# Late rows of the last two segments in the opening's pass, and three gate/up pairs moved into steps 58 to 60

## The chip, the cores and the metric

The kernel runs on one NeuronCore of a Trainium2 chip. The core has TensorE (PE, matrix products into PSUM), VectorE (DVE), ScalarE (ACT), GpSimd (POOL) and SyncE (SP), which here issues nearly all DMA transfers. The metric is the time of one execution on the device in microseconds. The profile is of one execution; its times count from the start of its span.

## The reference

Input x is 2048 rows of 640. The output is the sum of two residual parts:

```
h  = x + A(layernorm(x))
h2 = h + B(layernorm(h))
```

A is attention with a recurrent memory. The rows are cut into 64 segments of 32. Each segment is joined to 8 memory rows, and these 40 rows go through q, k and v products (32 heads of 128), masked softmax and the output product Wo. The first 8 output rows are the memory of the next segment, the other 32 are the segment's output. So the 64 segments follow one another strictly.

```
h = concatenate([mem, xs]);  q, k, v = h @ Wq, h @ Wk, h @ Wv
p = softmax(where(mask, q k^T * scale, -1e9));  o = (p @ v) @ Wo
mem = o[:8];  out = o[8:]
```

B is a gated feed-forward, `relu(x Wg) * (x Wu) @ Wd` with 1728 inner columns.

## The kernel before, in words

**Order.** The kernel lists its operations in program order with the buffers that each reads and writes (`add`, line 39). `solve` derives the waits, and each engine then runs its own operations in that order. SP is a queue too: a transfer that waits holds up all that SP has listed behind it.

**Segments and steps.** A PE pass has 32 columns of activations as its stationary operand, four column groups side by side, and streams the weights, 512 columns at a time: `project` (line 373), 40 matmuls for each of K, Q and V. Step s puts 8 memory rows and the first 24 rows of segment s into one pass. The other 8 rows of each segment, its late rows, do not wait for the memory. They are gathered for four segments at once in `act_e` (4 times 8 columns) and go through K, Q and V in a pass of their own. These passes are the filler of the steps: `extra_units` (line 797) gives each of three steps out of four one of the three passes for the next four segments, cut into three parts that PE runs between the products of the recurrence (`filler`, line 968); the fourth step runs the Wo product of late rows instead. Results go to `Ke`, `Qe` and `Ve`, two buffers each, used in turn by groups of four segments.

**Groups.** `place(s)` (line 454) gives buffer and column of a segment. Segments 0 and 1 are columns 2 and 3 of buffer 1, 2 to 5 are columns 0 to 3 of buffer 0, and so on; 62 and 63 are columns 0 and 1 of buffer 1. So the first and the last group hold two segments each, and half of their columns are empty. The opening (lines 727 to 778) normalises rows 0 to 63 (`ln1_load(-1)`), computes the first two groups while the weights arrive, and steps 58, 59 and 60 compute K, Q and V of the last.

**Fill.** `fill_of` (line 950) gives for each step a number of extra PE instructions: weight loads that could be left out, and 512-column matmuls cut in two. It changes no result.

**Feed-forward.** Rows are handled in four blocks of 512. `gate_up(b, j)` (line 847) is one pair: 5 gate and 5 up matmuls of 128 inner columns, a relu on ACT and a product on DVE into `hT`; 13 full pairs and a narrow tail (`Wt`) per block. `down_pair` (line 1145) is the product with Wd, two tiles of 128 rows at a time; its first part asks for `hT` chunks 0 to 11 and Wd pieces 0 to 3 at once. The weights of the feed-forward lie where Wq, Wk and Wv were, so they are loaded only from step 62 on, in pieces (`load_piece`, `load_down`), held in order by keys on `hT`. Block 0 needs no new attention rows: its normalised rows were written to DRAM (`xn2_d`) in steps 19 to 43 and are loaded at step 62. Its first four pairs are spread over step 63 and what follows, the others are in the loop at line 1217. That loop also runs the normalisation of block 1 (`ln2_front` on DVE and ACT, `ln2_back` as a DMA transpose on SP), starting at pair 5 (`at0`).

Of the kernel before, what the change touches and what calls it, by code (L numbers as in the profile page):

```python
# [146 lines left out]


def bass_sequential_preLN__memory_aug_recurrent_mem_tr__glu_gated_reglu__prompt_kernel(
    nc: bass.Bass,  # L150
    A_x: bass.AP,
    A_mem0: bass.AP,
    A_Wq: bass.AP,
    A_Wk: bass.AP,
    A_Wv: bass.AP,
    A_Wo: bass.AP,
    A_seg_len: bass.AP,
    B_x: bass.AP,
    B_W_gate: bass.AP,
    B_W_up: bass.AP,  # L160
    B_W_down: bass.AP,
    out: bass.AP,
):
    build_kernel(nc, A_x, A_mem0, A_Wq, A_Wk, A_Wv, A_Wo, A_seg_len, B_W_gate, B_W_up, B_W_down, out)


def build_kernel(nc, A_x, A_mem0, A_Wq, A_Wk, A_Wv, A_Wo, A_seg_len, B_W_gate, B_W_up, B_W_down, out):
# [20 lines left out]
    xn2_d = nc.dram_tensor("xn2_d", [128, DC, TB], BF16)  # L188
    attn_d = nc.dram_tensor("attn_d", [S, 4, DC * 32], BF16)

    es = ExitStack()
# [38 lines left out]
    Ko = ar.alloc("Ko", [128, H, 32], BF16)  # L230
    Ke = [ar.alloc(f"Ke{i}", [128, H, 32], BF16) for i in range(2)]
    Qo = ar.alloc("Qo", [128, H, M + SEG], BF16)
    Qe = [ar.alloc(f"Qe{i}", [128, H, 32], BF16) for i in range(2)]
    Ve = [ar.alloc(f"Ve{i}", [128, 8, VW], BF16) for i in range(2)]
    Vp = ar.alloc("Vp", [128, 8, VW], BF16)
# [32 lines left out]

    def ap(t, off, dims, p0=0, n=128):
        row = 1  # L270
        for s in t.shape[1:]:
            row *= s
        return bass.AP(t, p0 * row + off, [[row, n]] + dims)
# [148 lines left out]
    def n_rows(b):  # L422
        return 64 if b < 0 else min(128, S - 64 - 128 * b)

    def ln1_load(b, buf, key, eng="sp"):
        t0, n = (0, 64) if b < 0 else (64 + 128 * b, min(128, S - 64 - 128 * b))
        dma(buf[0:n, :], x_ap[t0:t0 + n, :], w=[key], eng=eng)

    def ln1_trans(b, buf, key, bk):
        transpose_rows(buf, key, 64 if b < 0 else min(128, S - 64 - 128 * b), bk)  # L430

    def ln1_back(b, src, r, eng):

        n = n_rows(b)

        def copy(dst, sl, w):
            if eng == "pool":
                add("pool", lambda p: p.tensor_copy(dst, sl), r=r, w=w)
            else:
                add("dve", lambda v: v.tensor_copy(dst, sl), r=r, w=w)  # L440
        if b < 0:
            for e in range(2):
                copy(act_r[1][:, 2 + e, :, M:32], src[:, :, SEG * e:SEG * e + RID], [("act", 1, "x", 2 + e)])
                copy(act_e[1][:, :, M * (2 + e):M * (3 + e)], src[:, :, SEG * e + RID:SEG * e + SEG], [("acte", 1)])
            return
        for j in range(n // SEG):
            copy(act_r[b % 2][:, j, :, M:32], src[:, :, SEG * j:SEG * j + RID], [("act", b % 2, "x", j)])
        for j in range(n // SEG):
            copy(act_e[b % 2][:, :, M * j:M * j + M], src[:, :, SEG * j + RID:SEG * j + SEG], [("acte", b % 2)])
# [3 lines left out]

    def place(s):
        return (s - 2) // 4 % 2, (s - 2) % 4

# [284 lines left out]

    row_stats(xt, ("xt",), 64)
    row_scale(xt, ("xt",), 64, xt, ("xt",))
    ln1_trans(-1, xt, ("xt",), P0)
# [29 lines left out]
    def first_values(chunks):  # L774
        for c in chunks:
            for (a, ks), bks in zip((PASSES[0], PASSES[2]), OB[2]):
                project(a, ks, 2, (0, 1), bks, (c,))
    first_values(range(2))

    GROUPS = ((0, 256), (256, 512), (512, 1024), (1024, 1536), (1536, FM))  # L780
    pieces = [(t, n, src, g, lo, hi) for g, (c0, c1) in enumerate(GROUPS)
              for n, (t, src) in enumerate(((Wg, B_W_gate), (Wu, B_W_up)))
              for lo, hi in (((0, 3), (3, DC)) if c1 - c0 == 512 else ((0, DC),))]

# [10 lines left out]
    WPARTS = (range(0, 8), range(8, 9), range(9, 16))  # L795

    def extra_units(s):
        p, r = 1 - place(s)[0], place(s)[1]
        if s == NSEG - 3:
            p = 1 - place(NSEG - 1)[0]  # L800
            j = 0
            a, ks = act_e[p], [("acte", p)]
        elif s < NSEG - 3 and r < 3:
            j = (1, 0, 2)[r]
            a, ks = act_e[p], [("acte", p)]
            if s < 0 or (s - 2) // 4 + 1 > (NSEG - 2) // 4:
                return None, None
        else:
            return None, None
# [140 lines left out]
    def fill_of(s):  # L950
        n = {1: 31, 2: 8, 57: 39, 61: 39, 62: 50, 63: 0}.get(s, FILL[s % 4])
        alone = min(n // 4, 3)
# [3 lines left out]
    for s in range(1, NSEG):  # L956
# [16 lines left out]
        if s > 0:  # L973
            a, ks = pass_act(s)
            held, parts = fill_of(s)
            for i in range(2):
                project(a, ks, 1, (i,), ((P2, P3)[i],), *WAYS[i], held=i == 1 and held[0], parts=parts[i])
# [48 lines left out]
        if last:  # L1026
# [4 lines left out]
            exp_x(s, 0)  # L1031
            gate_up(0, 0)
            scores(s, 1)
# [136 lines left out]
    def load_down(n):  # L1170
        lo, hi = 3 * n, min(3 * n + 3, FC - 1)
        r = [("Wdone", 1), ("hT", 0, n + 4)]
        dma(Wd[:, lo:hi, :], B_W_down[128 * lo:128 * hi, :].rearrange("(j p) d -> p j d", p=128), r=r, w=[("Wd", n)])
# [20 lines left out]
    rows(P3, s % 2, s - 1)  # L1194
    gate_up(0, 1)
    load_piece(("VM", 0, 3))
    load_piece(("hT", 0, 0))
    pv_x(s, P0)
# [3 lines left out]
    late_o(s)  # L1202
    load_piece(("hT", 0, 1))
    gate_up(0, 2)
    ln2_load(4)
    load_piece(("hT", 0, 2))
    load_piece(("hT", 0, 2))
    gate_up(0, 3)
    load_piece(("hT", 0, 3))
    load_piece(("hT", 0, 3))  # L1210
    rows(P2, (s + 1) % 2, s)
# [5 lines left out]
    for b in range(NBLK):  # L1217
        if 0 < b < NBLK - 1:
            for u in range(4):
                ln2_load(4 * (b + 1) + u)  # L1220
        at0 = 5 if b == 0 else 1
        for j in range(FC):
            if b or j > 3:
                gate_up(b, j)
            if b == 0 and 4 <= j < 7:
                load_piece(("hT", 0, j))
            if b == 0 and j in (5, 7):
                ln2_load(6 + (j - 5) // 2)
            if b == 0 and 4 <= j < 9:
                load_down(j - 4)  # L1230
            if b == 0 and j == 5:
                for q, src in enumerate((B_W_gate, B_W_up)):
                    for e in range(2):
                        r0 = FR * (q ^ e)
                        dma(Wt[:, e, :, r0:r0 + FR], src[:, FM:F].rearrange("(c p) f -> p c f", p=128),
                            r=[("Wdone", 0), ("hT", 0, 5)], w=[("Wt", q, e)])
            if b == 0 and j == 9:
                dma(h_rows[0][:, :, :], h_d[:, :].rearrange("(u p) d -> p u d", p=128), r=[("h_d", u) for u in range(4)] +
                    [("Wdone", 1), ("hT", 0, 9)], w=[("h", 0, u) for u in range(4)])
            if b + 1 < NBLK:  # L1240
                if j - at0 in (0, 2, 4, 6):
                    ln2_front(4 * (b + 1) + (j - at0) // 2)
                if j - at0 - 2 in (0, 2, 4, 6):
                    ln2_back(4 * (b + 1) + (j - at0 - 2) // 2, None)
        assert not pieces
# [65 lines left out]
```

## Time and profile before

| | |
|---|---|
| median of 3 runs | 1000.74 us (1000.2 to 1001.01) |
| the profiled execution | 999.84 us, span 998.1 us |
| one step (steps 2 to 60) | 11.9 to 12.3 us |
| opening, to the first matmul of step 1 | 56.8 us |
| steps 58, 59, 60, 61: first matmul at | 744.4, 756.4, 768.5, 780.5 us |
| step 63: first matmul at | 804.7 us |
| block 0: loop of pairs from, down product from | 826.1, 846.6 us |
| block 1: first pair at | 861.7 us |
| DMA moved | 73.3 MB, 44 GB/s from and to HBM over the span |

A row of the timeline is start, length, engine, line of the kernel, operation, tiles written and read, shapes and number. Matmuls overlap: the distance from start to start is what one costs, its length is the time until its last result. A row of the stage table is the stretch, its length, then busy time and instructions of PE, PEld (weight loads), DVE, ACT and POOL, the granted PE clock, the busy share of the DMA engines and GB/s. SPq is the time that SP takes to issue a transfer; the trace also records when each of a transfer's 16 parts landed.

### The profile page before, as it was taken

Reading aid. Unit: us, or ns where it says so; the run is one execution under the profiler, and the core shown is the slowest. Engines: PE = TensorE matmul, PEld = TensorE weight load, DVE = VectorE, ACT = ScalarE, POOL = GpSimd, SP = SyncE. Lnnn points to the kernel's source line nnn. Section 1 sums busy time; section 2 is a strip of 40 time slices with the busy share of each in tenths; the row PEclk is TensorE's granted clock in tenths of the full one; section 3 lists DMA queues with packets and bytes.
Section 4 is the critical chain, followed back from the end, with each engine's and each line's share of the span. In section 5 each row is a group of like instructions: output and inputs, shape, how many; then the busy total and the mean of one; then the engine's idle time right before and its main releaser. Section 6 shows DMA issues by size and latency. Waiting matters only on the chain.

```text
span 998.1 us, 56128 instructions
## 1 busy us (share of the span) xinstructions
PE 974.4 (98%) x26025; PEld 533.0 (53%) x24736; DVE 713.6 (71%) x1861; ACT 524.3 (53%) x1330; POOL 167.4 (17%) x414
## 2 busy tenths in 40 slices
PE   3899999999999999999999999999999999999998
PEld 1145555655555555555556565655555554344443
DVE  2568787878888887888788878787878766345332
ACT  0456666656666666666666566665656643122120
POOL 7021202021302130222022212121110010000000
PEclk9999999999999999999999999999999999999999
DMA  9931212121222122121212131112111169513100
GB/s 373 416 109 28 54 28 54 30 60 51 54 42 54 49 54 46 48 55 48 49 46 61 45 60 42 41 41 39 41 36 39 35 181 249 101 20 93 27 14 26
DMA packets 73534, 73.32 MB, mean 73 GB/s; under 512 B 42480, under 2 KB 60112, under 8 KB 71376
## 3 DMA queue, kind: packets, MB, share of 16 engines
q1 hardware_dynamic: 71568, 68.83, 25.0%
q8 instruction: 199, 3.26, 1.4%
q10 hardware_dynamic: 1728, 0.91, 0.3%
q14 instruction: 39, 0.32, 0.1%
HBM read 37.04 MB, written 6.55 MB: 44 GB/s over the span
## 4 chain that ended last, share of the span: by engine, by line
PE 94%; DMA 3%; DVE 1%; SPq 1%; issue 0%; ACT 0%; DVEq 0%; ACTq 0%
PE ps L394 47%; PE ps L858 11%; PE ps L367 8%; PE ps L582 7%; PE ps L599 7%; PE ps L642 4%; PE ps L1114 3%; DMA W<-in_A_Wv_dram 3%; PE ps L483 2%; PE ps L671 2%; PE ps L536 2%; SPq L332 1%; PE ps L871 0%; PE ps L1127 0%; PE ps L894 0%
## 5 line engine op out<-in xcount | busy, mean ns | idle before, releaser
L394 PE MATMUL ps<-W,act_r 128*32 128x512 bf16 (+1 forms) x8327 | 453.7, 357 | 1.7 <-ACT tok L418 0.9
L394 PEld LDWEIGHTS ps<-W,act_r 128*32 128x32 bf16 x8327 | 213.9, 96 | 165.7 <-DVE act_r L623 32.1
L418 ACT ACTIVATE tok<-ps 128x512 bf16<-128x512 f32 x190 | 109.3, 594 | 57.3 <-PE ps L394 48.7
L394 PE MATMUL ps<-W,act_e 128*32 128x512 bf16 x1224 | 119.5, 383 | 5.9 <-DVE TBf L464 3.4
L413 DVE STREAM_TRANSPOSE Ko<-tox 128x512 bf16<-128x512 bf16 x128 | 89.5, 700 | 40.1 <-ACT tox L418 39.7
L491 POOL COPY Qo<-Qe 128x256 bf16<-128x256 bf16 x64 | 27.8, 434 | 528.6 <-DVE oT L556 488.9
L418 ACT ACTIVATE tox<-ps 128x512 bf16<-128x512 f32 x134 | 79.6, 598 | 63.2 <-PE ps L394 42.5
L562 DVE STREAM_TRANSPOSE oT<-tox 128x512 bf16<-128x512 bf16 x128 | 95.6, 747 | 0.0
L413 DVE STREAM_TRANSPOSE Qo<-tok 128x512 bf16<-128x512 bf16 x124 | 85.5, 690 | 0.9
L367 PE MATMUL ps<-W,act_e 128*32 128x512 bf16 x856 | 84.1, 384 | 0.0
L582 PE MATMUL ps<-Wo,oT 128*32 128x160 bf16 x4032 | 81.4, 233 | 0.0
L599 PE MATMUL ps<-Wo,oT 128*32 128x320 bf16 x2016 | 79.8, 299 | 0.6 <-DVE rm L546 0.6
L582 PEld LDWEIGHTS ps<-Wo,oT 128*32 128x32 bf16 x4032 | 70.3, 97 | 11.0 <-DVE oT L556 3.1
L418 ACT ACTIVATE Vp<-ps 128x512 bf16<-128x512 f32 x127 | 75.2, 592 | 0.5 <-PE ps L858 0.5
L886 ACT ACTIVATE g<-ps 128x512 bf16<-128x512 f32 x52 | 30.1, 593 | 79.3 <-PE ps L858 79.3
L612 ACT ACTIVATE SA<-TA 64x40 f32<-64x40 f32 x126 | 29.5, 234 | 75.3 <-DVE TA L610 74.5
L499 ACT ACTIVATE Pm<-ps 128x64 bf16<-128x64 f32 x126 | 28.1, 223 | 73.0 <-PE ps L483 72.9
L858 PE MATMUL ps<-xn2T,Wg 128*128 128x512 bf16 x260 | 64.7, 380 | 0.0
L858 PE MATMUL ps<-xn2T,Wu 128*128 128x512 bf16 x260 | 64.6, 379 | 0.0
L887 DVE TENSOR_TENSOR hT<-g,ps 128x512 bf16<-128x512 bf16 x52 | 35.7, 686 | 40.3 <-PE ps L858 38.4
L599 PEld LDWEIGHTS ps<-Wo,oT 128*32 128x32 bf16 x2016 | 52.7, 97 | 16.8 <-DVE rm L546 1.3
L556 DVE STREAM_TRANSPOSE oT<-om 128x128 bf16<-128x128 bf16 x126 | 39.0, 310 | 31.1 <-ACT om L548 31.1
(114 smaller groups left out, 1447.0 us busy)
## 6 DMA issues: line engine op xcount, KB each, us to landing
VM<-Vp SPq DMA_DIRECT2D x126, 65.0 KB
VM<-Vp SPq DMA_DIRECT2D x63, 130.0 KB
W<-in_A_Wk_dram SPq DMA_DIRECT2D x5, 1024.0 KB
W<-in_A_Wq_dram SPq DMA_DIRECT2D x5, 1024.0 KB
W<-in_A_Wv_dram SPq DMA_DIRECT2D x5, 1024.0 KB
Wo<-in_A_Wo_dram SPq DMA_DIRECT2D x8, 640.0 KB
attn_d<-wtok SPq DMA_DIRECT2D x248, 7.5 KB
xt<-in_A_x_dram SPq DMA_DIRECT2D x16, 160.0 KB
```

Of the source, the lines that this page charges most:

```text
L367: return pe.add_instruction(mybir.InstMatmult(name=nc.get_next_instruction_name(), engine=mybir.EngineType.PE, ins=[pe.lower_ap(rhs), pe.l ...
L394: ins = pe.matmul(*b, start=(c == ends[0]), stop=(c == ends[1]), skip_group_check=True)
L413: add("dve", lambda v: v.transpose(dst[:, 16 * i:16 * i + 16, 0:32], tok[t][:, :].rearrange("p (h f) -> p h f", f=32)), r=tok_keys(t), w=keys)
L418: add("act", lambda a: a.activation(dst, src, ACTF.Copy), r=r, w=w)
L556: add("dve", lambda v: v.transpose(ap(oT[par], 160 * hf, [[40, 4], [320, 4], [1, 8]]), ap(om, 128 * hf, [[1, 4], [4, 32]])), r=[("om", hf) ...
L562: add("dve", lambda v, kh=kh: v.transpose(ap(oT[p], 160 * kh + M, [[320, 4], [40, 4], [1, 32]]), ap(tox, 128 * kh, [[256, 4], [1, 4], [4, ...
L582: i = pe.matmul(bank(bk)[32 * gg:32 * gg + 32, 0:160], src[:, hb, 0:32], w[:, gg], start=(hb == CH[16 * halves[0]]), stop=(hb == CH[-1]), ...
L599: i = pe.matmul(bank(bk)[32 * q:32 * q + 32, 0:320], src[:, hb, 0:32], w, start=(n == 0), stop=(n == 7), skip_group_check=True)
L642: ins = pe.matmul(bank(bk)[32 * q:32 * q + 32, 0:320], src[:, hb, 0:32], w[:, 2 * (q % 2):2 * (q % 2) + 2], start=(i == 0), stop=(i == 15) ...
L858: ins = pe.matmul(bank(bk), w[:, c, lo:lo + 128], xn2T[par][:, c, :], start=(c == 0), stop=(c == DC - 1))
L886: add("act", lambda a: a.activation(g1[gi][:, :], bank(bg), ACTF.Relu), r=[B(bg)], w=[("g1", gi)])
L887: add("dve", lambda v: v.tensor_tensor(hT[par][:, j, :], g1[gi][:, :], bank(bu), ALU.mult), r=[B(bu), ("g1", gi)], w=[("hT", par, j)])
```

## The change

The late rows of segments 62 and 63 are put into the 16 empty columns of the opening's first pass: `ln1_load(-1)` loads rows 0 to 63 and the last 64 rows together. `place` is changed so that segments 0 and 1 are columns 0 and 1 and segments 62 and 63 columns 2 and 3 of buffer 1. The results for all four lie in one tile, `ends`, which now holds buffer 1 of Ke, Qe and Ve (790 KB). It is written to DRAM at step 1, since groups in between use the same buffers, and loaded again at step 61.

Steps 58 to 60 no longer run the passes of the last group. They run three gate/up pairs of block 0, inner columns 0 to 383. At the top of step 58 SP loads the 512 normalised rows of block 0 (five transfers) into `ends`, which is free by then; at the top of each of the three steps it loads one 128-column piece of Wg into `xt` and one of Wu into `xl`. Part 0 of the filler is the whole gate product, part 1 one up matmul, part 2 the other four. The result goes through a free piece of `ends` to DRAM (`hx_d`) and into `hT` chunks 0 to 2 later, in block 0's loop. Block 0 then has ten full pairs and the tail after step 62 instead of 13 and the tail. The pieces of Wg and Wu are cut anew so that columns 0 to 383 come last. In block 0's loop what was tied to pair j is now tied to p = j - 3, and the normalisation of block 1 starts at p = 4 instead of 5. The fill of steps 58, 59 and 60 becomes 48, 96 and 100 (it was 7, 52 and 56).

```diff
     def n_rows(b):
-        return 64 if b < 0 else min(128, S - 64 - 128 * b)
+        return 128 if b < 0 else min(128, S - 64 - 128 * b)
...
     def place(s):
+        if s < 2 or s >= NSEG - 2:
+            return 1, s % 4
         return (s - 2) // 4 % 2, (s - 2) % 4
...
-    GROUPS = ((0, 256), (256, 512), (512, 1024), (1024, 1536), (1536, FM))
+    EC = 128 * NE
+    GROUPS = ((EC, EC + 256), (EC + 256, EC + 512), (EC + 512, EC + 1024), (EC + 1024, FM), (0, EC))
...
+    def early_rows(chunks):
+        for c in chunks:
+            t, k = XHOME[c]
+            dma(t, xn2_d[:, c, :], r=[("xn2_d", u) for u in range(4)], w=[k] + ([("Ve1", 1)] if c == DC - 1 else []))
+
+    def early_weights(j):
+        for t, k, src in ((xt, ("xt",), B_W_gate), (xl, ("xl",), B_W_up)):
+            dma(chunks_of(t[:, :]), src[:, 128 * j:128 * j + 128].rearrange("(c p) f -> p c f", p=128), w=[k])
+
+    def early_product(s, n):
...
+        def part(m):
+            mul(*((0, range(DC)), (1, range(1)), (1, range(1, DC)))[m])
+
+        def evac():
+            add("act", lambda a: a.activation(HOME, bank(BQ[0]), ACTF.Relu), r=[B(BQ[0])], w=[HKEY])
+            add("dve", lambda v: v.tensor_tensor(HOME, HOME, bank(BQ[1]), ALU.mult), r=[B(BQ[1]), HKEY], w=[HKEY])
+            dma(hx_d[:, n, :], HOME, r=[HKEY], w=[("hx", n)])
+        return part, evac
...
-        n = {1: 31, 2: 8, 57: 39, 61: 39, 62: 50, 63: 0}.get(s, FILL[s % 4])
+        n = {1: 31, 2: 8, 57: 39, 58: 48, 59: 96, 60: 100, 61: 39, 62: 50, 63: 0}.get(s, FILL[s % 4])
...
             held, parts = fill_of(s)
+            if NSEG - 6 <= s < NSEG - 3:
+                if s == NSEG - 6:
+                    early_rows(range(DC))
+                early_weights(s - NSEG + 6)
+            elif s == NSEG - 3:
+                dma(ends[:, :], ends_d[:, :], r=[("ends",)], w=END_KEYS)
+            elif s == 1:
+                dma(ends_d[:, :], ends[:, :], r=END_KEYS, w=[("ends",)])
...
-        at0 = 5 if b == 0 else 1
         for j in range(FC):
-            if b or j > 3:
+            p = j - NE if b == 0 else j
+            if b or p > 3:
                 gate_up(b, j)
-            if b == 0 and 4 <= j < 7:
+            if b == 0 and 4 <= p < 7:
                 load_piece(("hT", 0, j))
-            if b == 0 and j in (5, 7):
-                ln2_load(6 + (j - 5) // 2)
-            if b == 0 and 4 <= j < 9:
-                load_down(j - 4)
+            if b == 0 and p in (4, 6):
+                ln2_load(6 + (p - 4) // 2)
+            if b == 0 and 4 <= p < 9:
+                load_down(p - 4)
...
+            if b == 0 and p == 7:
+                dma(hT[0][:, 0:NE, :], hx_d[:, :, :], r=[("Wdone", 2), ("hT", 0, j)] + [("hx", n) for n in range(NE)],
+                    w=[("hT", 0, n) for n in range(NE)])
...
+                fronts, backs = ((4, 6, 8, 10), (6, 8, 9, 10)) if b == 0 else ((1, 3, 5, 7), (3, 5, 7, 9))
```

## The prediction

> **What bounds the kernel now.** First the page's busy rows and its chain of waits.
>
> ```profile
> PE 974.4 (98%) x26025; PEld 533.0 (53%) x24736; DVE 713.6 (71%) x1861; ACT 524.3 (53%) x1330; POOL 167.4 (17%) x414
> ...
> PE 94%; DMA 3%; DVE 1%; SPq 1%; issue 0%; ACT 0%; DVEq 0%; ACTq 0%
> ```
>
> TensorE (PE) is never idle for long, so a matmul taken away is worth its whole time, and any wait put in front of one costs its whole time. Next the PE timeline of step 58, whose filler the change replaces, and of the first feed-forward work in step 63.
>
> ```profile
> 751.81 0.22 PE L536 MATMUL ps<-Vp,Pbd 128*32 128x129 bf16 x4
> 751.86 0.39 PE L394 MATMUL ps<-W,act_e 128*32 128x512 bf16 x4
> 752.08 0.39 PE L367 MATMUL ps<-W,act_e 128*32 128x512 bf16 x4
> ...
> 808.64 1.25 PE L394 MATMUL ps<-W,act_r 128*32 128x512 bf16 x20
> 809.84 1.24 PE L858 MATMUL ps<-xn2T,Wg 128*128 128x512 bf16 x5
> 810.92 1.24 PE L858 MATMUL ps<-xn2T,Wu 128*128 128x512 bf16 x5
> 812.09 0.20 PE L483 MATMUL ps<-Qo,Ko 128*32 128x40 bf16 x4
> ```
>
> Starts are what to read: four column-tiled matmuls of the late-row pass start every 0.215 us (751.86, 752.08), and one full-array gate or up matmul also takes 0.216 us (five in 1.08 us, 809.84 to 810.92). A pass of 40 is ten times 0.215, a gate/up pair is ten times 0.216: equal. Step 58's filler is due at 751.86, 7.5 us after the step's start at 744.39.
>
> Then the SyncE (SP) queue, which issues nearly all transfers, and the stage table for block 0 of the feed-forward.
>
> ```profile
> 834.38 2.66 SPq L332 DMA_DIRECT2D Wt<-in_B_W_up_dram  x2
> 837.09 0.53 SPq L332 DMA_DIRECT2D Wu<-in_B_W_up_dram  x1
> ...
> 839.23 0.43 SPq L332 DMA_DIRECT2D Wd<-in_B_W_down_dram  x1
> ```
>
> ```profile
> 829.00:849.00 20.00, 20.00 (x106) 9.26 (x96) 14.12 (x31) 6.87 (x18) 0.00 (x0) 1.00 0.99 247
> ```
>
> ```profile
> 845.54 1.25 PE L871 MATMUL ps<-xn2T,Wt 128*128 128x256 bf16 x10
> 846.64 0.30 PE L1114 MATMUL ps<-Wd,hT 128*128 128x320 bf16 x1
> ```
>
> In the stage row the last two numbers are the DMA share, 0.99, and GB/s; the 20.00 before the first bracket is PE. PE and the DMA engines are both full from 829 to 849. The last row's down product starts at 846.64; by the trace's landing records the fourth piece of Wd (issued 839.23) landed at 844.68, the last at 847.43. The slack ahead of the down product is thus 2.0 us, and the change takes three pairs out of exactly this stretch.
>
> **The change part by part.**
>
> *Three gate/up pairs leave block 0 (A).* 3 x 2.16 = -6.5 us. The filler of steps 58 to 60 keeps its streaming time, ten times 0.216 in place of ten times 0.215. The fills (48, 96, 100) split matmuls: K in step 58 (fill 7) runs 744.39 to 746.66, in step 59 (fill 52) 756.42 to 758.70, the same length, so splits cost nothing here.
>
> *Opening (B).* 80 KB more of x ride ahead of the weights. The weight stream sets the opening (1 MB every 2.49 us by landings), so 82 KB cost 0.2 us; nothing if the early part has slack, 0.4 if paid twice. 128 rows instead of 64 change no instruction count in the normalisation; the copies lose one. Saving `ends` (790 KB) is issued at about 45 us, behind the weights already queued. The x load issued at 37.50 landed at 55.83, just behind the last Wo at 55.43, so the queue serves in order and the save ends near 58; the next transfer behind it is issued at 59.31. Zero; 1.9 us (790 KB at that rate) if it pushed in among the Wo pieces.
>
> *Rows and weights for step 58 (C).* SP gets to them after the two late-row stores that end at 747.88 (there the VM loads start at 747.92 now). Five row loads at 0.5 us each (like the xn2T loads of 798.27 to 800.31) and the gate piece then issues at 750.4. A 164 KB load in 256-byte pieces landed 2.75 us after its issue (831.35 to 834.11), so the gate weights land at about 753.2 and PE, in order, waits from 751.86: +1.4 us. Ends: 0.8 (landing in 2.2 us, as a small load) and 2.0 (3.5 us, as the 512-byte pieces at 807.42). Behind the waiting matmul stand the second memory product and with it the whole recurrence. The up weights, 0.5 us later, come before their matmul. VM loads of step 58 queue behind the seven new ones, to about 755, and are needed at 758.7: hidden. In steps 59 and 60 the hx store and two weight loads go out after the attention stores (758.85, 770.62), land near 762.7 and 774.5, needed at 763.9 and 776.0: hidden by 1.5 us, and that is all the cover. VectorE and ScalarE get less work than the pass's copies and flips (0.69 and 0.59 us for one product and one relu).
>
> *Restoring `ends` in step 61.* SP waits for the third hx store to land (785.1), which holds up nothing before the VM stores at 788.93. 790 KB then land near 789; GpSimd's copy for step 62 started at 790.57 and had 0.9 us to spare before its next task. Zero, cover 2.4 us.
>
> *Switching the array (D).* The 20 column-tiled matmuls at 808.64 take 1.20 us to the first full-array one instead of 1.08, the five at 810.92 take 1.17 to the next column-tiled one: 0.12 and 0.09 per switch. Each step's early pair is entered and left three times (before and after each part), 0.6 us at most; the old pass lost 0.09 at its own edges. One switch, from the 64-row product at 816.87, cost nothing. +0.4 a step, 1.2 in all (0.5 to 1.7).
>
> *The down product of block 0 (E).* Without waits it would start at 846.64 - 6.48 = 840.16. Its first part asks for Wd pieces 0 to 3 and now also for hT chunks 0 to 2, which the hx load brings. Times here leave out the shifts of B to D, which move PE and SP alike. SP: the piece at 829.20, two row loads, Wd 0 until 831.0. Then hT chunk 8, now behind the normalisation of tile 4, which comes one pair earlier (2.8 us on VectorE as at 831.24 to 834.04): 832.7 instead of 831.35. Wd 1 and the four Wt loads follow; the last of these sat 2.09 us on the queue at 834.95, and I let it be released at 836.5, when the load ahead of it has passed. Piece, two row loads and Wd 2 to 838.5, the transpose (1.26) to 839.8, Wd 3 at 839.85, hx at 840.35. A Wd load alone takes 3.8 us to land (829.63 to 833.41), under load 5.4. Data: from 831.1 the engines need 12.9 us for all this (1280-byte packets 56 ns, 1024-byte 46, 256-byte 18, 128-byte 12.5, over 16 engines), to 844.0 with no gap; before, the same sum gave 842.5 and Wd 3 landed at 844.68. With 1.7 us of gaps hx lands at 845.7: PE waits 5.6 us. Ends: 4.0 (no gaps) and 6.6 (2.2 of gaps and a late release).
>
> *PE after that wait (F).* The windows at the end of the span show the granted clock drop once PE is idle, (0.57, where 995 to 996 still had 1.00), and the opening shows the return.
>
> ```profile
> 997.90:998.10 0.20, 0.00 (x0) 0.00 (x0) 0.00 (x0) 0.00 (x0) 0.00 (x0) 0.57 0.00 0
> ```
>
> ```profile
> 17.16 0.62 PE L394 MATMUL ps<-W,act_e 128*32 128x512 bf16 x4 [3.40 <-DVE TBf L464]
> ...
> 21.40 0.55 PE L394 MATMUL ps<-W,act_e 128*32 128x512 bf16 x4
> 21.78 0.39 PE L367 MATMUL ps<-W,act_e 128*32 128x512 bf16 x4
> ```
>
> Matmuls ended at 995.2 and the clock was halved at 997.9, 2.7 us later; 1.67 us of idle at 40.26 changed nothing. In the opening groups started every 0.43 us until 21.7, 4.5 us after the work began, then every 0.215. So 5.6 us of idle brings half pace for up to 4.5 us: up to 2.3 lost, none if the drop just misses. I take 1.6, since most positions of the wait would be caught. [...]
>
> **Sum.** -6.5 + 0.2 + 1.4 + 1.2 + 5.6 + 1.6 = +3.5 us. The profiled execution has a span of 998.1 and a time of 999.84, 0.9 under the median of the runs, 1000.74; it goes to 1003.3, the median to 1004.2.
>
> **Rivals.** *The tail's transfers are hidden after all:* E and F vanish, -6.5 + 0.2 + 1.4 + 1.2 = -3.7, 997.0. For it: block 0 ran without a gap so far and half a megabyte of pieces got smaller. Against: a DMA share of 0.99 and SP at Wd 3 only at 839.2 even before. It decides if hx lands by 842: chance 0.12. *A short wait at full pace:* E 4.0, F 0, C 1.0, D 0.8: -0.5, 1000.2, no change; needs gapless DMA and the clock window to miss. 0.22, with all that ends within 2 us of before. *Restore or step weights late:* GpSimd's copy blocks the sum behind it in step 61 and with it the recurrence, 2 to 4 us on top: 1007. It decides if the restore lands more than 6.4 us after its issue; nothing of that size ran in this stretch. 0.06. The forecast keeps 0.60.
>
> **How the numbers follow.** About 0.2%, 2 us, is what this kernel's runs can tell. Faster is the first rival, 0.12; same the second, 0.22; slower the forecast (1002.8 to 1006.8) and the late restore, 0.66. The range, 999.0 to 1006.8, reaches into the second rival and leaves out 997.0 and 1007.
>
> **What would show it.** Right: no late-row pass in steps 58 to 60, and ten pairs and the tail in block 0; a PE gap of over 1 us before the first gate matmul of step 58, released by a DMA; a gap of 4 to 6.6 us before the first down matmul, released by the hx load or Wd; after it matmuls of 320 columns starting every 0.27 us instead of 0.135, with a granted clock under 1 in that stretch; block 1 unchanged. Wrong: the down product directly behind the tail, or a new gap in steps 61 and 62.

## The result, and the profile after

The changed kernel takes 1027.8 us (median of 4 runs, 1027.34 to 1030.66); beside it the kernel before took 1000.88 us (1000.2 to 1001.18). The ratio is 1.0276, 95% interval 1.0256 to 1.0296. The direction was forecast, the size was not: 1004.2 us, and at most 1006.8. The profiled execution took 1028.14 us with a span of 1026.4.

First the page's busy row and chain row.

```profile
PE 974.0 (95%) x25965; PEld 532.4 (52%) x24733; DVE 711.7 (69%) x1856; ACT 521.3 (51%) x1324; POOL 166.8 (16%) x412
...
PE 91%; DMA 4%; DVE 1%; SPq 1%; ACT 1%; issue 0%; POOL 0%; ACTq 0%; DVEq 0%; POOLq 0%
```

PE has the same busy time as before (974.4), although half clock (0.50 for 13.65 us in all) stretched some of its work; the 28.3 us of span are idle time. The chain gives about half of it to waits for DMA (4% of the span in place of 3%). A table by stage shows where. A step is counted from one `TBf` transpose on VectorE to the next (the transpose hands the new memory to the next step), the opening from the span's start to the first that ends step 0, the tail from the last one to the end.

| stage | before | after | difference |
|---|---|---|---|
| opening | 56.13 | 72.56 | +16.43 |
| steps 1 to 57, mean of a step | 12.06 | 12.07 | +0.4 in all |
| step 58 | 11.98 | 16.42 | +4.44 |
| steps 59, 60 | 12.04, 12.06 | 12.61, 12.60 | +0.57, +0.54 |
| steps 61, 62 | 12.03, 12.00 | 13.12, 11.96 | +1.09, -0.04 |
| tail | 194.24 | 199.11 | +4.87 |

**Opening.** VectorE's timeline (start, length, engine, line, operation, and in brackets the idle time ahead and what ended it), first the kernel before, then the changed one:

```profile
6.57 0.88 DVE L336 BATCH_NORM_STATS2 st<-xt 64x6 f32<-64x320 bf16 x2 [4.97 <-DMA xt<-in_A_x_dram]
```

```profile
25.69 0.89 DVE L353 BATCH_NORM_STATS2 st<-xt 128x6 f32<-128x320 bf16 x2 [24.09 <-DMA xt<-in_A_x_dram]
...
29.16 0.88 DVE L353 BATCH_NORM_STATS2 st<-oTe 128x6 f32<-128x320 bf16 x2
...
35.59 0.33 DVE L437 CAST ps<-wtok 128x160 f32<-128x160 bf16 x1 [2.06 <-DMA wtok<-in_A_mem_dram]
```

The joined x load is there at 25.67 us; before, the same statistics began at 6.57. What ScalarE's queue holds behind it is late as well: the next 128 rows land at 28.50 (before 9.43) and the memory rows at 35.56. Of those 128 rows, fourteen of the sixteen parts that the trace records were there by 10.35; only two were late.

**Step 58.** PE's timeline, then the stage table around it:

```profile
768.64 0.23 PE L558 MATMUL ps<-Vp,Pbd 128*32 128x129 bf16 x4
771.55 2.32 PE L840 MATMUL ps<-ends,xt 128*128 128x512 bf16 x5 [2.68 <-DMA xt<-in_B_W_gate_dram]
773.79 0.30 PE L558 MATMUL ps<-Ve,Pbd 128*32 128x129 bf16 x4
```

```profile
767.60:771.00 3.40, 1.27 (x60) 0.56 (x52) 2.35 (x9) 1.95 (x6) 0.00 (x0) 1.00 0.83 223
771.00:774.40 3.40, 2.85 (x14) 0.83 (x14) 0.15 (x1) 0.00 (x0) 0.00 (x0) 0.50 0.37 104
774.40:777.80 3.40, 3.40 (x101) 2.25 (x100) 1.87 (x7) 1.62 (x6) 1.12 (x3) 1.00 0.02 5
```

The gate product waits 2.68 us for its weights (issued 767.13, landed 771.50) and then takes 2.24 us from start to start (771.55 to 773.79), since the granted clock, the third number from the end, is 0.50 for 3.4 us.

**Steps 59 to 61.** Step 59's early pair at full clock, and the memory output of step 61:

```profile
785.29 0.23 PE L558 MATMUL ps<-Vp,Pbd 128*32 128x129 bf16 x4
785.45 1.25 PE L840 MATMUL ps<-ends,xt 128*128 128x512 bf16 x5
786.63 0.24 PE L558 MATMUL ps<-Ve,Pbd 128*32 128x129 bf16 x4
...
813.08 0.58 PE L604 MATMUL ps<-Wo,oT 128*32 128x160 bf16 x22
814.35 0.94 PE L604 MATMUL ps<-Wo,oT 128*32 128x160 bf16 x42 [0.69 <-issue]
```

The gate product is entered 0.16 us after the last column-tiled matmuls (they take 0.06 among themselves) and left after 1.18 instead of 1.08. In step 61 PE stops in the middle of an output product for 0.69 us with nothing that it waits for.

**Tail.** SP's issues, PE's timeline and the stage table:

```profile
860.31 1.79 SPq L349 DMA_DIRECT2D Wt<-in_B_W_up_dram  x1
...
865.49 1.00 SPq L349 DMA_DIRECT2D Wd<-in_B_W_down_dram  x1
866.53 0.48 SPq L349 DMA_DIRECT2D hT<-hx_d  x1
```

```profile
863.96 1.25 PE L928 MATMUL ps<-xn2T,Wt 128*128 128x256 bf16 x10 [1.31 <-DMA Wt<-in_B_W_up_dram]
871.82 0.42 PE L1179 MATMUL ps<-Wd,hT 128*128 128x320 bf16 x1 [6.60 <-DMA hT<-hx_d]
872.03 0.47 PE L384 MATMUL ps<-Wd,hT 128*128 128x320 bf16 x1
872.30 0.47 PE L1179 MATMUL ps<-Wd,hT 128*128 128x320 bf16 x1
```

```profile
840.00:860.00 20.00, 20.00 (x231) 10.24 (x230) 11.71 (x24) 6.26 (x15) 0.40 (x1) 1.00 0.80 232
...
863.20:866.50 3.30, 1.25 (x10) 0.90 (x10) 1.47 (x3) 1.32 (x4) 0.00 (x0) 1.00 0.78 195
866.60:876.80 10.20, 4.99 (x19) 1.43 (x10) 2.45 (x6) 0.50 (x2) 0.00 (x0) 0.50 1.02 285
```

Two waits, 1.31 for Wt and 6.60 for hx, and half clock until 876.8: matmuls of 320 columns start every 0.27 us. The tail's +4.87 is -6.3 for the three pairs (measured in the run with all edits, below), +7.9 for the waits, +2.5 for 5.0 us at half pace (871.82 to 876.82), and +0.7 between the last landing and the end of the span (1.70 us, before 1.01; 1.6 to 1.7 in every run with the change, for a reason that stays open).

### The profile page after: what moved, and what is told of

Its sections match the earlier page's. It is cut to its first block, busy times and chain, and to the rows that moved or that the text cites. A ratio compares the mean times of both kernels' runs of the same rounds, so it can differ in the third digit from the quotient of the medians.

```text
span 1026.4 us, 56072 instructions
## 1 busy us (share of the span) xinstructions
PE 974.0 (95%) x25965; PEld 532.4 (52%) x24733; DVE 711.7 (69%) x1856; ACT 521.3 (51%) x1324; POOL 166.8 (16%) x412
## 4 chain that ended last, share of the span: by engine, by line
PE 91%; DMA 4%; DVE 1%; SPq 1%; ACT 1%; issue 0%; POOL 0%; ACTq 0%; DVEq 0%; POOLq 0%
PE ps L411 45%; PE ps L915 9%; PE ps L384 8%; PE ps L604 7%; PE ps L621 7%; PE ps L664 4%; PE ps L1179 3%; DMA wtok<-in_A_mem_dram 3%; PE ps L505 2%; PE ps L693 2%; PE ps L558 2%; SPq L349 1%; PE ps L840 1%; DMA hT<-hx_d 1%; PE ps L928 0%
## 5 line engine op out<-in xcount | busy, mean ns | idle before, releaser
L411 PE MATMUL ps<-W,act_r 128*32 128x256 bf16 (+1 forms) x8396 | 454.4, 356 | 2.1 <-ACT tok L435 1.2
L435 ACT ACTIVATE tok<-ps 128x512 bf16<-128x512 f32 x186 | 107.2, 594 | 57.7 <-PE ps L411 48.8
L411 PE MATMUL ps<-W,act_e 128*32 128x512 bf16 x1152 | 112.6, 382 | 3.2 <-DVE TBf L486 3.2
L384 PE MATMUL ps<-W,act_e 128*32 128x512 bf16 x808 | 79.7, 384 | 0.0
L1179 PE MATMUL ps<-Wd,hT 128*128 128x320 bf16 (+4 forms) x225 | 59.8, 307 | 6.6 <-DMA hT<-hx_d 6.6
L505 PE MATMUL ps<-Qo,Ko 128*32 128x40 bf16 x2048 | 61.3, 181 | 0.0
L915 PE MATMUL ps<-xn2T,Wg 128*128 128x512 bf16 x245 | 61.0, 380 | 0.0
L915 PE MATMUL ps<-xn2T,Wu 128*128 128x512 bf16 x245 | 60.9, 379 | 0.0
```

Source lines behind the costliest of these rows:

```text
L384: return pe.add_instruction(mybir.InstMatmult(name=nc.get_next_instruction_name(), engine=mybir.EngineType.PE, ins=[pe.lower_ap(rhs), pe.l ...
L411: ins = pe.matmul(*b, start=(c == ends[0]), stop=(c == ends[1]), skip_group_check=True)
L435: add("act", lambda a: a.activation(dst, src, ACTF.Copy), r=r, w=w)
L505: i = pe.matmul(bank((P0, P1)[hf])[q:q + 32, o:o + 40], (Ko if a == 0 else Ke[p])[:, h, :], Qo[:, h, :], start=True, stop=True, skip_group ...
L915: ins = pe.matmul(bank(bk), w[:, c, lo:lo + 128], xn2T[par][:, c, :], start=(c == 0), stop=(c == DC - 1))
L1179: i = pe.matmul(*a, start=(j == 0), stop=(j == FC - 1), skip_group_check=True)
```

## The experiments

Three theories, one for each loss. Theory 1: the joined x load is slow because of its form, not its size. Theory 2: step 58 pays for loads that SP issues too late, and for the half clock behind that wait. Theory 3: the tail pays for what stands ahead of Wd 3 (the fourth piece of Wd) and hx (the load that brings the early pairs' result into `hT`) in SP's queue.

### One x load as two

```diff
-        src = bass.AP(A_x.tensor, 0, [[(S - 64) * D, 2], [D, 64], [1, D]]) if b < 0 else x_ap[t0:t0 + n, :]
+        if b < 0:
+            dma(buf[0:64, :], x_ap[0:64, :], w=[key], eng=eng)
+            dma(buf[64:128, :], x_ap[S - 64:S, :], w=[key + (1,)], eng=eng)
+            return
```

> The changed kernel with its first x load written as two loads of 64 rows each, nothing else. Theory 1, the joined load is served by two DMA engines alone because its outer size is 2, and each of its rows then stands behind one 8 KB weight packet: with two loads the rows land by 7 us as before the change, the end of step 0 comes back from 72.6 to 56.2-56.6 us, and the time falls from 1027.8 to 1011-1012. Rival, the 80 KB more or the 128 rows in the normalisation hold up the opening: step 0 still ends above 68 us, time above 1023. Steps 58 to 61 and the tail should stay as in the changed kernel (16.4, 12.6, 12.6, 13.1 and 199 us).

Measured: 1013.71 us (1011.39 to 1014.15), ratio to before 1.0122 (1.0106 to 1.0138). VectorE's timeline:

```profile
9.52 0.89 DVE L353 BATCH_NORM_STATS2 st<-xt 128x6 f32<-128x320 bf16 x2 [7.92 <-DMA xt<-in_A_x_dram]
...
57.06 0.35 DVE L647 STREAM_TRANSPOSE TBf<-ps 128x160 f32<-128x160 f32 x1 [5.36 <-PE ps L607]
```

15.5 of the 16.43 us come back with the same rows and bytes, so the rival falls. The second half lands at 9.49, later than I expected, and the opening keeps 0.9 us (and step 1 another 0.3). The tail was 200.8 here, 1.7 more than in the changed kernel, its wait 8.29; so the time is above the 1011 to 1012 expected.

### The kernel before with its load in two, and in four

Only the form of the 64-row load changes; some rows of the second segment are others than in the computation asked for.

```diff
-        dma(buf[0:n, :], x_ap[t0:t0 + n, :], w=[key], eng=eng)
+        src = bass.AP(A_x.tensor, 0, [[33 * D, 2], [D, 32], [1, D]]) if b < 0 else x_ap[t0:t0 + n, :]
+        dma(buf[0:n, :], src, w=[key], eng=eng)
```

> The kernel before with its 64-row first load written with an outer size of 2 (rows 0 to 31 and 33 to 64, so one row of the second segment is another one; the work is the same). It has the bytes and the arithmetic of before. Theory 1: two engines carry 32 rows each at one row per 0.33 us beside the weights, so the load lands at about 15.5 us in place of 6.6 and the opening is 8 to 10 us longer: 1009 to 1011. Rival, the form costs nothing and it was the size: 1000 to 1002.

The second run has `[[17 * D, 4], [D, 16], [1, D]]`.

> The kernel before with its first load written with an outer size of 4 (rows 0 to 15, 17 to 32, 34 to 49, 51 to 66, so 48 rows are others than before; the work is the same). Theory 1, the outer size of the transfer sets how many engines serve it: four engines carry 16 rows each at 0.33 us, the load lands at about 10 us (before 6.6, with an outer size of 2 14.8), and as the opening bears some 3 us of delay it ends within 1.5 us of before: 1000.5 to 1002.5. Rival, any load that is not one run of rows is slow: it lands near 14.8 us again and the time is near 1005.

Measured: 1004.94 us with an outer size of 2, ratio 1.0041 (1.0026 to 1.0056), and 1001.0 us with 4, ratio 1.0004 (0.9995 to 1.0013). The row statistics with 2, and the answer on VectorE's waits with 4 (total us, times, longest):

```profile
14.81 0.88 DVE L336 BATCH_NORM_STATS2 st<-xt 64x6 f32<-64x320 bf16 x2 [13.22 <-DMA xt<-in_A_x_dram]
```

```profile
DVE st L336 <- DMA xt<-in_A_x_dram: 8.2, 1, 8.2
```

The loads land at 14.79 and 9.80 us, as the row count per engine says (15.5 and 10). The trace has 16 landing records for the plain load (5.60 to 6.55 us) and two and four for these (and one more at 2.1 us, as the load is issued, long before rows land); I read each as one engine's. The time after the outer size of 2 was expected 4 to 6 us longer than it was: of 8.2 us of delay the opening took on 5.3 (it ends at 61.42). I had left out its slack of 3 us, which the expectation for 4 then used; with 4 the opening ends 1.76 us later than before (57.89), a little over the 1.5 expected.

### The joined load ahead of the weights

```diff
-    ln1_load(-1, xt, ("xt",), "act")
+    ln1_load(-1, xt, ("xt",))
```

> The changed kernel with its joined x load of 128 rows issued first on SP in place of ScalarE's queue, nothing else. It still runs on two engines, but stands ahead of the weights in the same queue. Theory 1 in full (each row waits for one weight packet of the other queue): without weights ahead the 64 rows of an engine take 64 x 0.055 = 3.5 us, the load lands at 6 to 7 us and the opening comes back to within 1 to 4 us of before (the weights of these two engines are 3.5 us late): 1012 to 1016. Rival, two engines are slow by themselves, 0.33 us a row whatever runs beside: it lands near 25 us and the time stays above 1025.

Measured: 1013.94 us, ratio 1.013 (1.0115 to 1.0146).

```profile
8.09 0.89 DVE L353 BATCH_NORM_STATS2 st<-xt 128x6 f32<-128x320 bf16 x2 [6.50 <-DMA xt<-in_A_x_dram]
```

The same two engines, with no weights ahead of the rows in their queue, are done at 8.07 (6 to 7 was expected) instead of 25.67; in return each of the first weight pieces lands 3.5 to 3.7 us after its first parts, and the opening ends at 58.88. So two engines are not slow by themselves, and what made the rows late was the weights of the other queue beside them. That each row waits for one weight packet rests on the rates: in the changed kernel 10 to 13 rows per 2 us pass between 10 and 27 us, on two engines one row in 0.31 to 0.4 us each; an 8 KB packet takes 0.33 us there and a row of 1280 bytes 0.06.

In the landing records of these runs an outer size of 2 gave two engines (the joined load: 25.54 and 25.67 us), one of 4 four, and the 64 rows in one run 16. Why the outer size sets the number, no run shows.

### Step 58's loads in step 57

Two x loads, and:

```diff
-            if NSEG - 6 <= s < NSEG - 3:
-                if s == NSEG - 6:
-                    early_rows(range(DC))
-                early_weights(s - NSEG + 6)
+            if NSEG - 5 <= s < NSEG - 3:
+                early_weights(s - NSEG + 6)
...
+        if s == NSEG - 7:
+            early_rows(range(DC))
+            early_weights(0)
         wo_split(par, P1)
```

> Two x loads as in the run with two loads, and the five row loads and the first pair's weights issued in step 57, ahead of its late-row stores, in place of the start of step 58. Theory 2, step 58 pays for rows and weights that SP issues too late, and then for half clock: its wait of 2.84 us and the half clock behind it both go, step 58 takes 12.6 in place of 16.4, 3.5 to 4.0 us less than the run with two loads (about 1007.5). Rival, the transfers are late because the engines are loaded there, not because of their place in the queue: the wait stays over 1.5 us and the gain is under 2 us.

Measured: 1009.72 us, ratio 1.0085 (1.0068 to 1.0102); step 58 took 14.21. The wait for weights is gone and the clock stays at 1.00, but PE has a new wait earlier in the step:

```profile
754.68 0.24 PE L561 MATMUL ps<-Ve,Pbd 128*32 128x129 bf16 x4 [1.56 <-DVE Pbd L530]
```

`Pbd` also holds the output rows of step 57, whose store to DRAM now stood behind the seven loads (issued 751.17 and 752.22, landed 754.19), and VectorE must not overwrite it before; it began at 754.27. Theory 2 had the cause right and forgot who else uses the queue. Of the 4.0 us gained over the run with two loads only 2.2 are from step 58; 1.5 are a shorter tail.

The mended order spreads the loads: gate weights at the start of step 57, four rows ahead of its VM loads, the fifth row and the up weights where all seven were; the second 64 rows of x go out on SP ahead of the weights.

> The opening and step 57 as in the run with all edits, the rest, block 0 among it, as in the changed kernel. Theory: step 58 takes 12.6 us, the opening ends at 56.3 to 56.8 and the tail keeps its wait of 6 to 7 us and its half clock (198 to 201 us): 1006 to 1008. Rival, step 58 needs its 2 us whatever the order, since the rows and weights meet the stores of the memory rows: step 58 at 14 us or above, time above 1008.

Measured: 1007.87 us, ratio 1.0073 (1.0059 to 1.0087), step 58 12.43, opening 56.74, tail 199.21. That is as theory 2 has it; only the tail's wait, 7.6 us (below), is longer than the 6 to 7 expected.

### Block 0: all of the order, and two parts of it

Two x loads, and:

```diff
+    dma(hT[0][:, 0:NE, :], hx_d[:, :, :], r=[("Wdone", 2)] + [("hx", n) for n in range(NE)], ...
     rows(P2, (s + 1) % 2, s)
...
-        r = [("Wdone", 1), ("hT", 0, NE + n + 4)]
+        r = [("Wdone", 1), ("hT", 0, NE + n + 3)]
...
-            if b == 0 and 4 <= p < 7:
+            if b == 0 and p in (9, 10):
+                load_piece(("hT", 0, j))
                 load_piece(("hT", 0, j))
...
-            if b == 0 and 4 <= p < 9:
-                load_down(p - 4)
+            if b == 0 and 3 <= p < 8:
+                load_down(p - 3)
```

> Two x loads, and another order of the transfers in block 0: the hx load goes out before the last memory rows, each Wd load one pair earlier, and the four pieces with columns 0 to 383, which only block 1 reads, after Wd and the h rows. Theory 3, the 6.6 us wait at the down product comes from what stands ahead of Wd 3 and hx in the queue: the wait falls under 1 us, with it the half clock, and the wait of 1.3 us for Wt gets shorter; 9 to 11 us less than the run with two loads (1001 to 1003). Rival, the DMA engines are simply full from 855 to 873 us and the bytes have to pass whatever their order: over 3 us of wait and some half clock remain, gain 2 to 5 us.

Measured: 1004.78 us, ratio 1.004 (1.0025 to 1.0055), 8.9 less than the run with two loads, a little short of the 9 to 11 expected; the tail 191.17 in place of 200.81.

```profile
850.45 0.30 PE L1182 MATMUL ps<-Wd,hT 128*128 128x320 bf16 x1 [2.62 <-DVE hT L941]
```

```profile
845.50:848.90 3.40, 2.33 (x16) 1.37 (x14) 2.31 (x6) 1.36 (x4) 0.00 (x0) 1.00 0.86 214
849.00:852.30 3.30, 1.85 (x14) 0.77 (x8) 2.31 (x6) 0.72 (x3) 0.00 (x0) 1.00 1.14 251
```

The wait for Wt is gone, and of 8.29 us ahead of the down product 2.62 are left (under 1 was expected), without half clock. (The row names VectorE, which was done at 850.32; Wd 3 landed at 850.36.) The rest: Wd 3 still stood behind the four Wt loads, of which two sat 1.09 and 1.77 us on the queue, and two row loads.

The two parts by themselves, on the run with step 58 mended:

> The run with step 58 mended and block 0 as in the changed kernel, but the four pieces with columns 0 to 383 moved behind the h rows; hx and Wd keep their places. It tells how much of the tail's 7.6 us wait these 983 KB are. Theory, they are the larger part: without them Wd 3 and hx go out 1 to 2 us earlier and need 2.3 to 3 us less of the engines: the wait falls to 3 to 5 us, one half window less or more, tail 194.5 to 196.5 in place of 198.9, time 1003.5 to 1005.5. Rival, the pieces pass in gaps of the stream and cost Wd nothing: wait over 6.5 us, time above 1006.5.

> The run with step 58 mended and block 0 as in the changed kernel, but the hx load issued before the last memory rows; pieces and Wd keep their places. Theory, hx landed 1.4 us after Wd 3 and its 393 KB, moved forward, use engines that are half idle there: the wait of 7.6 us falls by 1.0 to 2.0 us, tail 197 to 198 and time 1005.5 to 1007. Rival, the hx load alone makes the wait: it falls under 3 us, time under 1003.5.

Measured: 1005.79 us, ratio 1.0053 (1.0038 to 1.0068), with the pieces last; 1006.21, ratio 1.0064 (1.0048 to 1.0081), with hx early; without either 1007.87. PE's longest wait in the three, in the order neither, pieces, hx:

```profile
PE ps L1187 <- DMA hT<-hx_d: 7.6, 1, 7.6
```

```profile
PE ps L1187 <- DMA hT<-hx_d: 6.1, 1, 6.1
```

```profile
PE ps L1187 <- DMA Wd<-in_B_W_down_dram: 5.9, 1, 5.9
```

The hx load did what theory 3 expected. The pieces did not: the wait fell by 1.5, not by 2.6 to 4.6. Neither alone is the cause. Added up they save 3.3 us of wait; the whole order, which also issues each Wd load a pair earlier, took 5.7 from a wait of 8.29. So a large part of the wait is a queue that reached Wd 3 and hx too late, held by keys on `hT` and by Wt. That is by difference: no run moves the Wd loads alone.

### All edits, and fewer switches

Mended step 57 and opening, hx early, Wt one pair earlier, Wd 2 and 3 in one pair and Wd 4 in the next, row loads of tile 7 behind Wd 4, pieces last, and the restore of `ends` split: its Ke and Qe part goes out at the end of step 60 ahead of the last hx store.

> All edits together, and each put where the runs so far say. The second 64 rows of x go out on SP ahead of the weights. In step 57 the first pair's gate weights go out at its start, four rows ahead of its VM loads, the fifth row and the up weights after its second memory product; so the stores of the rows of that step stay in time, which they did not in the run with all seven loads in one place. The hx load goes out before the last memory rows, Wd 2 and 3 in one pair, Wt one pair earlier, the four pieces for block 1 last. The restore of ends is split in two, its first part a little earlier. Theory: what is left is -6.5 for the three pairs, +0.2 for the opening, 3 x 0.55 for the switches of the array, 0.3 to 0.6 in steps 61 and 62, 0 to 0.5 in the tail: 996 to 998, step 58 at 12.6 us and no wait over 0.5 us ahead of the down product, PE at full clock from 41 us to the end. Rival: each wait taken away is replaced by another of its size, the DMA engines being full in block 0; then the tail stays above 190 us and the time at 1000 or above.

Measured: 997.05 us (996.78 to 998.81), ratio to before 0.9965 (0.9951 to 0.9978). The down product follows the tail product directly:

```profile
843.81 1.25 PE L931 MATMUL ps<-xn2T,Wt 128*128 128x256 bf16 x10
845.06 0.30 PE L1189 MATMUL ps<-Wd,hT 128*128 128x320 bf16 x1
845.19 0.30 PE L384 MATMUL ps<-Wd,hT 128*128 128x320 bf16 x1
```

Step 58 takes 12.44 and the tail 188.48. The rival, that the engines are full anyway, falls. The profiled execution is the longest of the five (998.81): its opening ends at 58.74, against 56.74 with the same code in the run with only step 58 mended, because a piece of Wv came later and PE stood 2.58 us and then ran at half clock from 41.2 to 44.7. So the full clock from 41 us on, which was expected, did not come in this execution; the time did.

Then the up product in one part, and with it the second half of x back on ScalarE's queue:

```diff
-            mul(*((0, range(DC)), (1, range(1)), (1, range(1, DC)))[m])
+            if m != 1:
+                mul(m // 2, range(DC))
```

> The run with all edits, but the up product of each early pair in one part, after the memory output, with no single matmul between the second memory product and the output: two switches of the array less a step. Theory, a switch costs 0.1 us whatever stands around it: 0.2 us less in each of the steps 58 to 60 (12.4 in place of 12.6), 996.4. Rival, the single matmul covers the normalisation of the second memory product: PE then waits 0.3 to 0.5 us for it and the steps take 12.7 or more, 997.4 to 998.

> The run with the up product in one part, with the second 64 rows of x back on ScalarE's queue behind the first 64. Theory, ahead of the weights the rows shift the whole weight stream and the opening ends at 59.1 us (both runs with all edits); on ScalarE's queue it ends at 57.1 to 57.4, as in the three runs that had it so, with 0.3 us more in step 1: 995 to 996. Rival, the two ways are equal and 59.1 was chance, since the run with the opening on SP and the old block 0 ended it at 57.1: 996.5 to 997.2.

Measured: 996.82 us, ratio 0.9961 (0.9948 to 0.9975), and 997.4, ratio 0.9973 (0.9962 to 0.9983). Steps 58 to 60 take 12.21, 12.56, 12.57 in the first. Step 58 is 0.23 shorter, but a matmul has only moved behind its end: step 61 is 0.23 longer (12.43, before 12.20). Steps 59 and 60 are 0.04 shorter, where two switches at 0.1 should have given 0.2. The memory output that now follows the second memory product directly runs 1.26 us instead of 1.10 to the next product, which eats most of the gain; neither theory had that. The tail is 0.8 longer (189.30), for a new wait of 0.81 ahead of the down product. The place of the second x load makes no difference that these runs can tell: the opening ends at 56.79 with it on ScalarE's queue and at 58.79 with it on SP, but steps 1 and 62 are 0.3 longer each, and the profiled execution on SP is again the longest of its five (999.48). The 995 to 996 of the theory did not come; 997.4 is nearer the rival, just over its range. (The 59.1 and 57.1 of that expectation count to the transpose's end, 0.35 later.)

## Why the prediction was right in sign and wrong in size

**B, opening: +0.2 forecast, +16.43 measured. This is the step that failed**, and 16 of the 24 us that the forecast fell short. It priced the extra rows as bytes, 82 KB at the rate of the weight stream, with an upper end of 0.4. I looked at how many bytes the new load has and not at how its addresses are written: a leading dimension of two in place of one run of rows. The runs with outer sizes of 2 and 4, and the one with the joined load on SP, show that this makes it, beside the weights of the other queue (14.79 and 9.80 us for 64 rows, 25.67 for the joined 128, 8.07 for them ahead of the weights). The extra rows themselves cost more than the 0.2 to 0.4 forecast: with two loads the opening is 0.5 to 0.9 us longer in seven runs, and 2.6 in the profiled executions of two others. The sign does not hang on B: with two loads the kernel is still slower than before, 1013.71 us.

**A, three pairs out of block 0: -6.5 forecast, -6.3 measured.** In the run with all edits the down product starts 36.10 us after the last transpose of the steps, before 42.42.

**C, wait in step 58: +1.4 forecast, 4.0 measured** (4.44 less 0.46 of switches). SP issued the gate weights just when the sum had it, at 767.13, which is 750.3 on the clock of before (the step starts 16.8 us later). What was mis-sized is their way: 4.37 us to landing in place of 2.75. Yet fifteen of the sixteen parts were there after 2.82 us; one came 1.55 later. The same holds for the fifth row load ahead of it (2.39 and 4.20), and in all four runs with these loads in step 58 the last part of the gate weights took 3.7 to 4.4 us. A 16 KB packet of the queue that the trace calls `instruction` was on the move at that time (from 768.59, for 0.93 us). The records do not name the engine of a packet, so why one part was late stays open. The half clock behind the wait, 1.3 us, was not in the sum at all. The wait of 2.68 filled 0.63 of one window of 3.41 us and the clock was halved; the 1.4 that I expected fills at most 0.41 of one, and none of the 27 windows with 0.31 to 0.53 was followed by half clock (last section).

**D, switches: +1.2 forecast, 0.46 + 0.57 + 0.54 = 1.6 measured** (step 58 taken from the run with it mended), inside 0.5 to 1.7. Taking two of six switches away did not give back their part.

**Restore of `ends`: 0 forecast, up to +1.09 in step 61.** It landed at 812.99, 0.14 before GpSimd's copy from it (813.13) where 2.4 of cover was forecast, and the sum behind that copy was not held up. What cost time was the 0.69 us stop of PE without a named reason, after the restore's packets had passed: a new gap in step 61, one of the signs of being wrong that the prediction named. It fell on the same matmul, the 23rd of 64, for 0.35 us in the run with all loads in step 57 and for 0.39 in the one with the joined load on SP, and not in step 61 of the five other runs with the restore in one piece. The trace has 199 packets of 16 KB on its `instruction` queue, one for some 255 of PE's matmuls and weight loads, so I take them to be PE's. One of them moved from 812.1 to 813.0. In the eight runs with the restore in one piece this packet began 9.40 to 9.88 us after step 60's last transpose in the three where PE stopped, and 8.88 to 9.05 in the five where it did not; before the change it was 7.84, and 7.80 to 8.14 in the three runs with the restore in two. Each stop ended 2.25 to 2.4 us after the packet's start, and so did one of 0.38 us in step 62 of the run with the pieces last, behind a later packet. That the packet stood behind the restore, and PE waited for it, fits all this but is argued, not shown: no run varied the restore alone. What the other 0.4 us of step 61 are (0.2 to 0.4 in every run with the change) stays open too.

**E, wait ahead of the down product: 5.6 forecast (4.0 to 6.6), 6.60 and 1.31 measured.** The mechanism, its place and its releaser were right. What was mis-sized is Wt: I let the last of its four loads be released in time for the tail product, and it landed 1.2 us after PE wanted it (863.87 against 862.65). It left SP's queue at 862.10, which is 838.7 on the clock of before (the tail starts 23.4 us later), where I had 836.5; so Wd 3 and hx went out 2.2 and 2.8 us later than in the sum. That the queue more than the engines makes the wait was only half in my sum, which counted 12.9 us of data from 831.1 and 1.7 of gaps. (The 56 ns of a 1280-byte packet in that sum is the usual one; the mean from 831 to 845 before the change was 65.5, so part of the gaps is slow packets.)

**F, half pace after it: 1.6 forecast, 2.5 measured.** The 320-column matmuls start every 0.27 us, as said. The clock stayed at 0.50 for 10.24 us, three windows of 3.41: the wait filled the first of them and 0.53 of the second, and full clock came back after the third, which was all busy. That most positions of the wait would be caught, from which I took 1.6, and that the clock window might miss, as the second rival had it, was my estimate; no run shows how many positions are caught. What the runs show in its place are windows of 3.41 us in which the position counts: half clock followed 2.58 us with 2.15 in one of them, and did not follow 2.62 us that lay over two (last section).

The rivals: the tail's transfers were not hidden, the short wait did not come, the restore was late by little. Without B's miss the sum of the measured terms would have been about +11.9, 1012.6, still above the range, for C, E and F each came out at or over its upper end. I had given each its middle, though F hangs on E, and both on the same queue, so that they go wrong together.

## What to carry to other kernels

When a transfer is rewritten, look at the leading dimension of its address pattern before its bytes; here joining two ranges into one pattern left the load to two engines, and it landed at 25.67 us where two transfers of the same rows had landed by 9.49. When work moves to an earlier place, list what its loads stand ahead of in their queue, stores included, and place each load at its own earliest point: here that turned +27 us into -3.6. See how a wait on PE lies in the windows of the clock: here 2.58 and 2.68 us, which filled 0.63 of one window of 3.41 us, were followed by half clock, while after 2.37 and 2.62 us, which filled at most 0.53 of one, it stayed at 1.00.

## What the runs showed of the hardware that was not expected

**In these runs the clock followed the idle share of a window.** In the traces the granted clock changes only at borders 3.41 us apart (771.01 to 774.42, and 10.24 us = three of them in the tail; the changed kernel's stretches at full clock, 730.45, 92.16 and 150.19 us, are 214, 27 and 44 of them). I took each window at full clock of the kernel before, the changed one and the twelve runs, and the share of it in which no matmul ran. Twelve windows had a share of 0.63 or more (five of them 0.63), and the clock was halved after every one; 27 had 0.31 to 0.53, and it was halved after none. (The windows before the clock first rose and around the end of each run are left out; they agree.) Between 0.53 and 0.63 there was none. Two runs lie on either side of this gap: the 2.68 us wait of step 58 filled 0.63 of one window and was followed by 0.50 (above); in the run with the joined load on SP the same wait was 2.37 us, filled 0.53, and the clock stayed:

```profile
753.50:756.90 3.40, 1.59 (x80) 0.76 (x72) 2.67 (x10) 1.98 (x6) 0.00 (x0) 1.00 0.60 156
757.00:760.30 3.30, 2.84 (x49) 1.50 (x52) 0.79 (x3) 0.37 (x1) 0.21 (x1) 1.00 0.62 180
```

So the clock stayed at 1.00 after 2.62 us that fell on two windows (0.33 and 0.44, the run with the new order of block 0), and was halved after 2.58 us of which 2.15 fell on one (the run with all edits). From half clock it came back after each of the twelve windows with a share of 0.16 or less, and after none of the twelve with 0.30 or more. What on the chip counts the idle time, the traces do not show.

**Taking out switches between column-tiled and full-array matmuls gained less than their price.** They cost 0.1 us each in the timeline of step 59, but only 0.04 a step was gained in steps 59 and 60 when two of six were removed, since the output product behind them took 0.16 longer. Why it did stays open.
